# Attention and a feed-forward block on one core: late weight conversions ranked by their block, not in front of the late sweeps

## The chip, the cores and the metric

The kernel runs on one core of one Trainium2 chip. The metric is the device time of one execution in microseconds (us), median of several runs. A core has TensorE (PE, matrix products), VectorE (DVE) and ScalarE (ACT) for element work, GpSimd (POOL), and SyncE (SP), whose queue issues most of the transfers (DMA).

## What is computed

The reference, cut to its core (B = 4, H = 8, S = 1152, D = 64; 2304 tokens, model width 512, inner width 2048):

```python
q_pool = q.reshape(B, H, S // 2, 2, D).mean(axis=3)
scores = scale * np.matmul(q_pool, k.transpose(0, 1, 3, 2))
scores = scores - np.max(scores, axis=-1, keepdims=True)
attn = np.exp(scores)
attn = attn / (np.sum(attn, axis=-1, keepdims=True) + 1e-09)
x = np.matmul(attn, v)          # then heads side by side: 2304 x 512
h = x @ w_in
g = np.maximum(h, 0.0) + alpha * np.minimum(h, 0.0)
out = g @ w_out
```

## The kernel before

The first part of the program is the attention: 32 heads, each in 9 chunks of keys. Its results x go to DRAM (xs) as a high and a low half, since products are made of three matmuls in a reduced float format: high by high, high by low, low by high (`mm3`, L395).

The second part is the feed-forward block. Its inner width is cut into 16 blocks of 128 (f = 0 to 15), the tokens into 8 groups of 288 (4 batches, j = 0 or 1). For one block and one group, `hidden` (L403) makes h on PE (12 matmuls), then ACT makes pos = relu(h) and neg = relu(-h), DVE joins them with alpha (L424, called pos below), ACT rounds that to gs' high half (L430) and DVE subtracts to get the low half (L435, called gs below). With gs, PE makes y, another 12 matmuls. The low sweeps (`low_sweep`, 8 of them, blocks 0 to 4) run beside the attention and put partial sums yp into DRAM; the late or high sweeps (`high_sweep`, 8 of them, blocks 5 to 15) come after it, add up y in four PSUM banks and add yp on DVE (ys, L492). Late sweep 0 reads its x from tiles xh, late sweep 1 from tiles x.

The weights arrive as 64-bit floats, 512 KB for half a block (i = 0 is w_in, i = 1 is w_out; "half block 11.0" is block 11 with i = 0). `w_convert` (L328) turns a half block into two tiles wh and wl: a load on SP into one of two wraw tiles (L332), one step on ACT (L335), four on DVE (top L338, tail L344, sign L350, value L356), a rounding copy on ACT (wh, L317) and a subtraction on DVE (wl, L320). Blocks 0 to 4 are converted during the attention, blocks 5 to 7 at its end into tiles that the attention no longer needs, and blocks 8 to 15 (16 half blocks) after it.

The order on every engine is made when the program is built, by a list scheduler (`Scheduler`). It keeps a planned time for every engine; of the tasks that could start within a slack of the earliest one (about 200 ns on ACT and DVE, none on PE) it takes the one with the smallest `prio`. On the chip each engine then works through its own list in that order. Late sweep s has prio 2000 + s, and block f in it 0.05 (f - 5) more; y comes 0.23 behind its h. The late conversions get `2 * FF + 0.05 * (f - NLO) - HW` (L1104, FF = 1000, NLO = 5). A `lock` lets only one DVE or POOL task of a group be planned at a time.

Of the kernel before, what the change touches and what calls it, by code (L numbers as in the profile page):

```python
# [13 lines left out]
AF = mybir.ActivationFunctionType  # L14
ALU = mybir.AluOpType
# [7 lines left out]
PE, ACT, DVE, POOL, SP = range(5)  # L23
# [159 lines left out]
def attention_ffn(  # L183
# [49 lines left out]
    SWITCH: int = 9,  # L233
    GL: float = 3.5,
    COL: float = 0.099,
    HW: float = 1.0,
    XB: int = 5,
    REUSE: int = 6,
    XH: int = 1,
    RP: float = 31.0,  # L240
# [4 lines left out]
    nc = tc.nc  # L245
    NH, D, S = kt.shape
    SQ = qt.shape[4]
    B = out.shape[0]
    H = NH // B
    P = 128  # L250
    NC = S // P
    HQ = SQ // 2
# [5 lines left out]
    DMO = KD * P  # L258
# [7 lines left out]
    def act(n, psum=False):  # L266
        return n / 1.2 + (50 if psum else 93)
# [12 lines left out]
    add = sch.add  # L280
# [4 lines left out]
    nal = const.tile([P, NFF], F32, tag="nal", name="nal")  # L285
# [39 lines left out]
        add(DVE, dve(DMO), low, reads=[mag], writes=[w], deps=[t], prio=prio, lock=True)  # L325
        w_done[f, i] = w

    def w_convert(f, i, prio, release=(), ring=None, left=()):  # L328
        raw, mag, bits = Buf(r_raw), Buf(r_mag), Buf(r_bits)

        def load():
            nc.sync.dma_start(out=raw.t.rearrange("p n t -> p (n t)"), in_=wt[f, i].bitcast(I32))  # L332

        def size():
            nc.scalar.activation(out=mag.t, in_=raw.t[:, :, 1].bitcast(F32), func=AF.Abs)  # L335

        def top():
            nc.vector.tensor_scalar(  # L338
                out=bits.t, in0=raw.t[:, :, 1], scalar1=3, scalar2=0x3FFFFFF8,
                op0=ALU.logical_shift_left, op1=ALU.bitwise_and,  # L340
            )

        def tail():
            nc.vector.scalar_tensor_tensor(  # L344
                out=bits.t, in0=raw.t[:, :, 0], scalar=29, in1=bits.t,
                op0=ALU.logical_shift_right, op1=ALU.bitwise_or,
            )

        def sign():
            nc.vector.scalar_tensor_tensor(  # L350
                out=bits.t, in0=raw.t[:, :, 1], scalar=-0x40000000, in1=bits.t,
                op0=ALU.bitwise_and, op1=ALU.bitwise_or,
            )

        def value():
            nc.vector.scalar_tensor_tensor(  # L356
                out=mag.t, in0=mag.t, scalar=F64_TINY, in1=bits.t.bitcast(F32),
                op0=ALU.is_ge, op1=ALU.mult,
            )

        add(SP, 600, load, writes=[raw], prio=prio - 1, size=P * DMO * 8)
        t0 = add(ACT, act(DMO), size, reads=[raw], writes=[mag], prio=prio)
        t1 = add(DVE, dve(DMO) * 0.6, top, reads=[raw], writes=[bits], deps=release, prio=prio, lock=True)
        t2 = add(DVE, dve(DMO), tail, reads=[raw], writes=[bits], deps=[t1], prio=prio, lock=True)
        t3 = add(DVE, dve(DMO), sign, reads=[raw], writes=[bits], deps=[t2], prio=prio, lock=True)
        add(DVE, dve(DMO), value, reads=[bits], writes=[mag], deps=[t0, t3], prio=prio, lock=True)
        w_split(f, i, mag, prio, ring, left)


    nal_b = Buf()  # L370
# [32 lines left out]
    def hidden(f, x, prio):  # L403
        ps, pos, neg, gs = Buf(r_h), Buf(r_pos), Buf(r_neg), Buf(r_gs)
        t = None
        for kd in range(KD):

            def mm(kd=kd):
                mm3(ps.t, f, kd * P, lambda hl: x[kd].t[:, hl, :], kd == 0, kd == KD - 1)

            t = add(PE, 396, mm, reads=[x[kd], w_done[f, 0]], writes=[ps], deps=[t] if t else [], prio=prio,
                    kind="group" if kd else "first")
        add(
            ACT, act(HQ, True), lambda: nc.scalar.activation(out=pos.t, in_=ps.t[:, :HQ], func=AF.Relu),  # L414
            reads=[ps], writes=[pos], prio=prio,
        )
        add(
            ACT, act(HQ, True),
            lambda: nc.scalar.activation(out=neg.t, in_=ps.t[:, :HQ], func=AF.Relu, scale=-1.0),  # L419
            reads=[ps], writes=[neg], prio=prio,  # L420
        )
        t = add(
            DVE, dve(HQ),
            lambda: nc.vector.scalar_tensor_tensor(  # L424
                out=pos.t, in0=neg.t, scalar=nal[:, f:f + 1], in1=pos.t, op0=ALU.mult, op1=ALU.add
            ),
            reads=[neg, pos, nal_b], writes=[pos], prio=prio, lock=True,
        )
        t = add(
            ACT, act(HQ), lambda: nc.scalar.activation(out=gs.t[:, 0], in_=pos.t, func=AF.Copy),  # L430
            reads=[pos], writes=[gs], deps=[t], prio=prio,
        )
        add(
            DVE, dve(HQ),
            lambda: nc.vector.tensor_tensor(  # L435
                out=gs.t[:, 1], in0=pos.t, in1=gs.t[:, 0].bitcast(F32), op=ALU.subtract
            ),
            reads=[pos], writes=[gs], deps=[t], prio=prio, lock=True,
        )
        return gs  # L440
# [92 lines left out]
    pair_qs = [None]  # L533
# [20 lines left out]
                deps=deps[i], uses=[k1], writes=[k3_b[n]], prio=n - 2, size=D * S * 2,  # L554
            )

    loads = []

    def head_prep(n):
        kk, k1, q1 = Buf(r_kk), Buf(r_k1), Buf(r_q1)  # L560
        i = n % 2
        if n >= 2:
            if i == 0:
                pair_qs[0] = Buf(r_qs)
                load = add(
                    SP, 600, lambda qs=pair_qs[0]: nc.sync.dma_start(out=qs.t, in_=qt[n // 2, 0]),
                    writes=[pair_qs[0]], prio=n - Q0, size=P * 2 * SQ * 4,
                )
                add(
                    POOL, 1050,  # L570
                    lambda qs=pair_qs[0]: nc.gpsimd.dma_start(out=qs.t, in_=qt[n // 2, 1], accum_op=ALU.add),
                    writes=[pair_qs[0]], deps=[load], prio=n - Q1, size=P * 2 * SQ * 4, dma=True,
                )
            qs, qc = pair_qs[0], i
        else:
            qs, qc = Buf(r_qs), 0
            add(
                SP, 600, lambda: nc.sync.dma_start(out=qs.t, in_=qt[n // 2, :, :, i].rearrange("t d q -> d t q")),
                writes=[qs], prio=n - 2.6, size=P * 2 * SQ * 4,
            )  # L580
            eng, dur, e = pair_op(P1, SQ)
            add(
                eng, dur,
                lambda e=e: e.tensor_tensor(out=qs.t[:, 0], in0=qs.t[:, 0], in1=qs.t[:, 1], op=ALU.add),
                reads=[qs], writes=[qs], prio=n - 1.6,
            )
        for j in range(2):
            d = slice(j * D, (j + 1) * D)
            add(
                SP, 600, lambda d=d: nc.sync.dma_start(out=kk.t[d], in_=kt[n]), writes=[kk], prio=n - KL,  # L590
                size=D * S * 4,
            )
        halves(n, qs, qc, [qs.writers[-1]] * 2, n - KR)
        add(
            ACT, act(SQ), lambda: nc.scalar.activation(out=q1.t, in_=qs.t[:, qc], func=AF.Copy),
            reads=[qs], writes=[q1], prio=n - KR,
        )
        q_rest[n] = qs, qc
        add(
            ACT, act(S), lambda: nc.scalar.activation(out=k1.t, in_=kk.t, func=AF.Copy),  # L600
            reads=[kk], writes=[k1], prio=n - KR + 0.1,
        )
        loads.append(k1.writers[-1])
        key_halves(n, k1, [k1.writers] * 2)
        add(
            ACT, act(SQ),
            lambda: nc.scalar.activation(
                out=q2[n % 2][:D, PAD:], in_=q1.t[:D].bitcast(F32), func=AF.Copy
            ),
            reads=[q1], writes=[q2_b[n]], deps=old_users(n), prio=n - 0.5,  # L610
        )
        add(
            DVE, dve(S),
            lambda: nc.vector.tensor_tensor(  # L614
                out=k2[n % 2][:D], in0=kk.t[:D], in1=k1.t[:D].bitcast(F32), op=ALU.subtract
            ),
            reads=[kk, k1], writes=[k2_b[n]], deps=old_users(n) + late * (n == 1), prio=n - KS, lock=True,
        )
        return k1, q1
# [13 lines left out]
    first_q2, first_k2, first_load, late, maxed = Buf(), Buf(), [None], [], {}  # L633
# [374 lines left out]
    with ExitStack() as actx:  # L1008
# [9 lines left out]
        with ExitStack() as pctx:  # L1018
# [37 lines left out]
            for n in range(0, NH, 2):  # L1056
# [4 lines left out]
            t = add(SP, 600, lambda: nc.sync.dma_start(out=nal, in_=alpha), uses=[], writes=[nal_b], deps=[first_load[0]], prio=3)  # L1061
            add(
                DVE, 100,
                lambda: nc.vector.tensor_scalar(out=nal, in0=nal, scalar1=-1.0, scalar2=None, op0=ALU.mult),
                writes=[nal_b], deps=[t], prio=3,
            )
            for i in range(2):
                for f in range(NLO):
                    r = int(R2 + R3 * f if i else R0 + R1 * f)
                    w_convert(f, i, W2 + W3 * f if i else W0 + W1 * f, [maxed[max(0, r)]])  # L1070
            rings = [r for r in (r_kk, r_qs, r_k1) for i in range(2)]
            for c in range(REUSE):
                f, i = NLO + c // 2, c % 2
# [83 lines left out]
```

## Time and profile before

| | us |
|---|---|
| median of 3 runs (lowest, highest) | 898.33 (897.49, 900.25) |
| the profiled execution | 899.73 |
| its span, first to last instruction | 898.0 |
| PE busy | 873.2 (97%) |
| DVE busy | 622.7 (69%) |
| ACT busy | 514.2 (57%) |
| POOL busy | 171.3 (19%) |

A stage is judged by its own windows: the share of a whole span mixes the attention, in which all engines work, with the late sweeps, in which PE is nearly alone. The attention's last writes of x are issued at 553 to 556 us; late sweep 0 begins on PE at 606.25 us.

### The profile page before, as it was taken

What the parts mean: (1) busy time and instruction counts of PE and PEld (TensorE: products, weight loads), DVE (VectorE), ACT (ScalarE), POOL (GpSimd) and SP (SyncE); (2) the same over time, 40 slices, a digit from 0 to 9 for tenths busy, and PEclk for the clock granted to TensorE, in tenths of its full rate; (3) what the DMA queues carried; (4) which work ended last, traced back from release to release, by engine and by line L of the source; (5) the groups of instructions that cost most, each with busy time, mean ns of one, the idle gap of its engine ahead of it and who ended that gap; (6) DMA issues with size and microseconds to landing.
All of it is one profiled execution on the core that took longest, in us unless ns stands there. A gap on an engine that the chain in (4) does not pass through costs nothing.

```text
span 898.0 us, 16880 instructions
## 1 busy us (share of the span) xinstructions
PE 873.2 (97%) x6273; PEld 742.6 (83%) x6273; DVE 622.7 (69%) x984; ACT 514.2 (57%) x1337; POOL 171.3 (19%) x126
## 2 busy tenths in 40 slices
PE   8799899999999999999999999999899999999998
PEld 5576666677778778777777789999799999999998
DVE  6899999977887688787798972588833243243332
ACT  5577677767676677666676664565533243333432
POOL 3332333333332332333322320000000000000000
PEclk9799999999999999999999999999899999999999
DMA  9757678685755765674463435774313113112000
GB/s 261 192 153 183 161 174 221 154 223 127 186 160 131 181 171 135 152 197 131 114 148 96 115 106 146 295 229 132 118 53 107 54 54 107 53 54 93 1 27 27
DMA packets 59496, 121.71 MB, mean 136 GB/s; under 512 B 12795, under 2 KB 25622, under 8 KB 59414
## 3 DMA queue, kind: packets, MB, share of 16 engines
q1 hardware_dynamic: 57254, 111.79, 43.5%
q0 software_dynamic: 2160, 8.85, 5.6%
q8 instruction: 49, 0.80, 0.4%
q14 instruction: 33, 0.27, 0.1%
HBM read 92.36 MB, written 19.02 MB: 124 GB/s over the span
## 4 chain that ended last, share of the span: by engine, by line
PE 79%; DVE 16%; ACT 2%; issue 2%; DMA 1%; SPq 0%; POOL 0%; DVEq 0%; ACTq 0%; POOLq 0%
PE h L398 28%; PE y L398 15%; PE av L920 12%; PE s L879 7%; PE m L811 7%; PE s L880 6%; DVE bx L828 4%; PE s L942 2%; DVE acc L908 2%; DVE wmag L356 1%; DVE wl L320 1%; DVE wbits L344 1%; DVE wbits L350 1%; PE av L1043 1%; DVE k L614 1%
## 5 line engine op out<-in xcount | busy, mean ns | idle before, releaser
L892 ACT ACTIVATE p<-s 128x288 f32<-128x288 f32 x576 | 204.9, 409 | 81.1 <-PE s L880 77.1
L908 POOL TENSOR_TENSOR acc<-acc,p 128x576 f32<-128x576 f32 x96 | 151.2, 1575 | 346.6 <-ACT p L892 159.0
L828 DVE TENSOR_REDUCE bx<-m 128x2 f32<-128x768 f32 x192 | 179.9, 949 | 36.6 <-PE m L811 35.4
L879 PE MATMUL s<-q,k 128*128 128x288 f32 x576 | 171.2, 311 | 1.0 <-ACT p L892 0.8
L880 PE MATMUL s<-q,k 65*128 65x288 f32 x576 | 165.2, 300 | 0.0
L920 PE MATMUL av<-p,vv 128*64 128x288 f32 x1152 | 162.3, 417 | 0.0
L424 DVE SCALAR_TENSOR_TENSOR pos<-neg,nal,pos 128x288 f32<-128x288 f32 x128 | 66.7, 526 | 109.7 <-ACT neg L419 104.9
L879 PEld LDWEIGHTS s<-q,k 128*128 128x128 f32 x576 | 110.2, 191 | 22.4 <-issue 12.0
L414 ACT ACTIVATE pos<-h 128x288 f32<-128x288 f32 x128 | 51.3, 404 | 124.2 <-PE h L398 124.1
L920 PEld LDWEIGHTS av<-p,vv 128*64 128x64 f32 x1152 | 74.6, 137 | 55.8 <-issue 16.9
L398 PE MATMUL h<-x,wh 128*128 128x288 f32 x576 | 117.8, 297 | 0.0
L811 PE MATMUL m<-k,q 128*128 128x384 f32 (+1 forms) x384 | 106.3, 363 | 6.1 <-DVE q L627 3.6
L880 PEld LDWEIGHTS s<-q,k 65*128 65x128 f32 x576 | 110.4, 192 | 0.1
L398 PE MATMUL y<-gs,wh 128*128 128x288 f32 x512 | 105.6, 300 | 3.2 <-DVE gs L435 3.2
L398 PEld LDWEIGHTS h<-x,wh 128*128 128x128 f32 x576 | 92.3, 188 | 2.9 <-issue 2.7
L435 DVE TENSOR_TENSOR gs<-pos,gs 128x288 fp32r<-128x288 f32 x128 | 58.8, 463 | 46.0 <-ACT gs L430 45.6
L430 ACT ACTIVATE gs<-pos 128x288 fp32r<-128x288 f32 x128 | 56.2, 443 | 59.7 <-DVE pos L424 59.3
L398 PEld LDWEIGHTS y<-gs,wh 128*128 128x128 f32 x512 | 84.1, 192 | 3.7 <-DVE gs L435 3.7
L398 PE MATMUL h<-x,wl 128*128 128x288 f32 x288 | 84.8, 294 | 0.0
L811 PEld LDWEIGHTS m<-k,q 128*128 128x128 f32 (+1 forms) x384 | 62.7, 196 | 26.2 <-issue 10.0
L908 DVE TENSOR_TENSOR acc<-p 128x576 f32<-128x576 f32 x96 | 72.3, 754 | 10.9 <-ACT p L892 9.7
L398 PE MATMUL y<-gs,wl 128*128 128x288 f32 x256 | 76.5, 299 | 0.0
(97 smaller groups left out, 1263.5 us busy)
## 6 DMA issues: line engine op xcount, KB each, us to landing
kk<-kt SPq DMA_DIRECT2D x63, 288.0 KB
wraw<-wt SPq DMA_DIRECT2D x32, 512.0 KB
x<-xs SPq DMA_DIRECT2D x48, 288.0 KB
qs<-qt SPq DMA_DIRECT2D x16, 576.0 KB
vv<-vt SPq DMA_DIRECT2D x32, 288.0 KB
xs<-x SPq DMA_DIRECT2D x64, 144.0 KB
k<-k SPq DMA_DIRECT2D x62, 144.0 KB
qs<-qt POOLq DMA_DIRECT2D x15, 576.0 KB, 7.2
```

Source lines behind the costliest of these rows:

```text
L398: nc.tensor.matmul(out=ps[:, :HQ], lhsT=w[a, c // DMO][:, c % DMO:c % DMO + P], rhs=lo(hl), start=(first and i == 0), stop=(last and i == 2),)
L414: ACT, act(HQ, True), lambda: nc.scalar.activation(out=pos.t, in_=ps.t[:, :HQ], func=AF.Relu),
L424: lambda: nc.vector.scalar_tensor_tensor(out=pos.t, in0=neg.t, scalar=nal[:, f:f + 1], in1=pos.t, op0=ALU.mult, op1=ALU.add),
L430: ACT, act(HQ), lambda: nc.scalar.activation(out=gs.t[:, 0], in_=pos.t, func=AF.Copy),
L435: lambda: nc.vector.tensor_tensor(out=gs.t[:, 1], in0=pos.t, in1=gs.t[:, 0].bitcast(F32), op=ALU.subtract),
L811: nc.tensor.matmul(out=ms.t[:, i, :JW], lhsT=q1.t[d, PAD + t * P:PAD + (t + 1) * P], rhs=k1.t[d, j * JW:(j + 1) * JW], start=True, stop=True,)
L828: lambda c=c, e=e, step=step, m=len(pair), ms=ms: nc.vector.tensor_reduce(out=bx.t.rearrange("p t j -> p (t j)")[:, c:e + 1:step], in_=ms. ...
L879: nc.tensor.matmul(out=ps.t[:, :HQ], lhsT=k1.t[:, s], rhs=q1.t[:, q], start=True, stop=False)
L880: nc.tensor.matmul(out=ps.t[:, :HQ], lhsT=k2[n % 2][:, s], rhs=q2[n % 2][:, PAD + q.start:PAD + q.stop], start=False, stop=True)
L892: lambda ps=ps, p=p, h=h: nc.scalar.activation(out=p.t[:, h], in_=ps.t[:, :HQ], func=AF.Exp, scale=SCALE),
L908: lambda a=a, b=b, part=part, e=e: e.tensor_tensor(out=part.t, in0=a.t, in1=b.t, op=ALU.add),
L920: nc.tensor.matmul(out=av.t[h * D:(h + 1) * D, :HQ], lhsT=vv.t[:, e], rhs=p.t[:, h], start=(e == 0), stop=(e == NC - 1),)
```

## The change

HW goes from 1.0 to 0.1. Before, the conversions of blocks 8 to 15 had prio 1999.15 to 1999.5, ahead of everything in the late sweeps (2000 and up). Now block f's conversion has 1999.9 + 0.05 (f - 5), which is 0.1 or two blocks ahead of its own use in late sweep 0 (2000 + 0.05 (f - 5)). Loads have 1 less. Three options are new (QA, LD, NT); at their default values they leave the old branches in place, and nal gets a second operation, an addition of 0.0.

```diff
-    HW: float = 1.0,
+    HW: float = 0.1,
     XB: int = 5,
+    QA: float = 1.0,
+    LD: int = 0,
+    NT: int = 0,
...
-        add(SP, 600, load, writes=[raw], prio=prio - 1, size=P * DMO * 8)
+        add(SP, 600, load, writes=[raw], deps=first if f == 0 else (), prio=prio - 1, size=P * DMO * 8)
...
+        if not NT:
+            add(
+                ACT, act(HQ, True), lambda: nc.scalar.activation(out=pos.t, in_=ps.t[:, :HQ], func=AF.Relu),
+                reads=[ps], writes=[pos], prio=prio,
+            )
...
-                out=pos.t, in0=neg.t, scalar=nal[:, f:f + 1], in1=pos.t, op0=ALU.mult, op1=ALU.add
+                out=pos.t, in0=neg.t, scalar=nal[:, f:f + 1], in1=ps.t[:, :HQ] if NT else pos.t, op0=ALU.mult, op1=ALU.add
             ),
-            reads=[neg, pos, nal_b], writes=[pos], prio=prio, lock=True,
+            reads=[neg, ps if NT else pos, nal_b], writes=[pos], prio=prio, lock=not NT,
...
-                add(
+                q_sums[n // 2] = add(
                     POOL, 1050,
                     lambda qs=pair_qs[0]: nc.gpsimd.dma_start(out=qs.t, in_=qt[n // 2, 1], accum_op=ALU.add),
-                    writes=[pair_qs[0]], deps=[load], prio=n - Q1, size=P * 2 * SQ * 4, dma=True,
+                    writes=[pair_qs[0]], deps=[load], prio=n - Q1, size=int(QA * P * 2 * SQ * 4), dma=True,
...
-                lambda: nc.vector.tensor_scalar(out=nal, in0=nal, scalar1=-1.0, scalar2=None, op0=ALU.mult),
+                lambda: nc.vector.tensor_scalar(
+                    out=nal, in0=nal, scalar1=-1.0, scalar2=1.0 if NT else 0.0, op0=ALU.mult, op1=ALU.add
+                ),
...
-                    w_convert(f, i, W2 + W3 * f if i else W0 + W1 * f, [maxed[max(0, r)]])
+                    w_convert(f, i, W2 + W3 * f if i else W0 + W1 * f, [maxed[max(0, r)]], first=[q_sums[1]] if LD else ())
```

The lists of all engines are the same up to the end of the attention. Three places differ. In the new kernel's list the line numbers are 3 to 7 higher.

On SP, at the first weight loads of the late blocks (wraw), the list of before and the list of the change read:

```order
L462 DMA yp_0_81<-ys 128x288 x2
L332 DMA wraw<-wt 128x1024
L462 DMA yp_0_81<-ys 128x288
L332 DMA wraw<-wt 128x1024
L391 DMA xh<-xs_73 128x576
L462 DMA yp_0_81<-ys 128x288
L391 DMA x<-xs_76 128x576
L391 DMA xh<-xs_73 128x576 x3
L470 DMA ypt<-yp_0_77 128x1152
```

```order
L467 DMA yp_0_81<-ys 128x288 x2
L394 DMA xh<-xs_73 128x576
L467 DMA yp_0_81<-ys 128x288
L394 DMA xh<-xs_73 128x576 x2
L467 DMA yp_0_81<-ys 128x288
L394 DMA x<-xs_76 128x576
L394 DMA xh<-xs_73 128x576
L335 DMA wraw<-wt 128x1024 x2
L475 DMA ypt<-yp_0_77 128x1152
```

Both weight loads have moved behind the four loads of xh and one of x.

On DVE, behind the last step of half block 11.0 (wl11_0), where late sweep 0 begins (pos_7974 is block 5's, the next number block 6's), before and after:

```order
L320 TENSOR_TENSOR wl11_0_7945<-wmag_7894,wh11_0_7944 128x512
L338 TENSOR_SCALAR wbits_7986<-wraw_7887 128x512
L344 SCALAR_TENSOR_TENSOR wbits_7986<-wraw_7887,wbits_7986 128x512
L350 SCALAR_TENSOR_TENSOR wbits_7986<-wraw_7887,wbits_7986 128x512
L356 SCALAR_TENSOR_TENSOR wmag_7984<-wmag_7984,wbits_7986 128x512
L424 SCALAR_TENSOR_TENSOR pos_7974<-neg_7979,nal_68,pos_7974 128x288
L424 SCALAR_TENSOR_TENSOR pos_7996<-neg_8001,nal_68,pos_7996 128x288
L320 TENSOR_TENSOR wl11_1_8024<-wmag_7984,wh11_1_8023 128x512
L338 TENSOR_SCALAR wbits_8042<-wraw_7928 128x512
L344 SCALAR_TENSOR_TENSOR wbits_8042<-wraw_7928,wbits_8042 128x512
```

```order
L323 TENSOR_TENSOR wl11_0_7945<-wmag_7918,wh11_0_7944 128x512
L429 SCALAR_TENSOR_TENSOR pos_7974<-neg_7979,nal_68,pos_7974 128x288
L341 TENSOR_SCALAR wbits_7990<-wraw_7870 128x512
L440 TENSOR_TENSOR gs_7992<-pos_7974,gs_7992 128x288
L347 SCALAR_TENSOR_TENSOR wbits_7990<-wraw_7870,wbits_7990 128x512
L429 SCALAR_TENSOR_TENSOR pos_7998<-neg_8004,nal_68,pos_7998 128x288
L353 SCALAR_TENSOR_TENSOR wbits_7990<-wraw_7870,wbits_7990 128x512
L440 TENSOR_TENSOR gs_8019<-pos_7998,gs_8019 128x288
L359 SCALAR_TENSOR_TENSOR wmag_7985<-wmag_7985,wbits_7990 128x512
L429 SCALAR_TENSOR_TENSOR pos_8024<-neg_8032,nal_68,pos_8024 128x288
```

The hidden blocks' steps have moved in between the steps of half block 11.1. From here to the last step of half block 15.1 the list held 18 of them (pos or gs); it holds 24 now.

On PE, around the h of one of the last blocks of late sweep 0, before (wl_1_8133 and wh_1_8234 are half blocks 12.1 and 13.1, wh_0_8356 is 15.0) and after (wh_1_8275 and wh_0_8333 are 13.1 and 14.0, and h from x is late sweep 1):

```order
L398 MATMUL y<-gs,wl_1_8133 128x288
L398 MATMUL h<-xh,wh_0_8356 128x288 x2
L398 MATMUL h<-xh,wl_0_8357 128x288
L398 MATMUL h<-xh,wh_0_8356 128x288 x2
L398 MATMUL h<-xh,wl_0_8357 128x288
L398 MATMUL h<-xh,wh_0_8356 128x288 x2
L398 MATMUL h<-xh,wl_0_8357 128x288
L398 MATMUL h<-xh,wh_0_8356 128x288 x2
L398 MATMUL h<-xh,wl_0_8357 128x288
L398 MATMUL y<-gs,wh_1_8234 128x288 x2
```

```order
L401 MATMUL h<-xh,wh_0_8333 128x288 x2
L401 MATMUL h<-xh,wl_0_8334 128x288
L401 MATMUL y<-gs,wh_1_8275 128x288 x2
L401 MATMUL y<-gs,wl_1_8276 128x288
L401 MATMUL h<-x,qs 128x288 x9
L401 MATMUL h<-x,k_6829 128x288 x12
L401 MATMUL h<-x,wh_0_7493 128x288 x2
L401 MATMUL h<-x,wl_0_7494 128x288
```

Before, two hidden blocks of late sweep 1 stood ahead of late sweep 0's last y. Now seven and a quarter stand there, spread over the last blocks, and behind that y comes sweep 1's first y at once; before, three of sweep 1's hidden blocks stood between.

## Rows read from the trace of the kernel before

**Rows 1.** The page's 40 slices: the TensorE clock that was granted, in tenths.
```profile
PEclk9799999999999999999999999999899999999999
```

**Rows 2.** Windows by stage: busy PE, PEld, DVE, ACT, POOL; clock, DMA, GB/s.
```profile
550.00:600.00 50.00, 50.00 (x380) 50.00 (x379) 30.21 (x64) 28.85 (x74) 0.00 (x0) 1.00 0.73 243
...
610.00:650.00 40.00, 35.95 (x245) 35.11 (x245) 35.76 (x68) 21.97 (x54) 0.00 (x0) 0.91 0.37 114
...
700.00:880.00 180.00, 180.00 (x1363) 180.00 (x1362) 63.42 (x133) 63.27 (x171) 0.00 (x0) 1.00 0.17 55
```

**Rows 3.** Windows of 2 us behind the last conversions of late sweep 0.
```profile
638.00:640.00 2.00, 0.00 (x1) 0.01 (x1) 1.85 (x5) 0.40 (x2) 0.00 (x0) 0.79 0.00 0
640.00:642.00 2.00, 2.00 (x8) 2.00 (x9) 1.97 (x4) 1.41 (x4) 0.00 (x0) 0.50 0.02 4
```

**Rows 4.** PE's waits from 550 to 660 us: total us, times, longest us.
```profile
PE y L398 <- DVE gs L435: 3.2, 2, 3.0
PE h L398 <- ACT neg L419: 0.9, 1, 0.9
```

**Rows 5.** PE's timeline: start, us, operation, idle time before and its releaser.
```profile
606.25 1.75 PE L398 MATMUL h<-xh,kk 128*128 128x288 f32 x12
...
640.00 0.61 PE L398 MATMUL y<-gs,wh 128*128 128x288 f32 x1 [2.98 <-DVE gs L435]
...
645.68 0.57 PE L398 MATMUL h<-xh,wh 128*128 128x288 f32 x2
...
652.20 1.75 PE L398 MATMUL h<-x,k 128*128 128x288 f32 x12
```

**Rows 6.** DVE's timeline: steps with other work between them, then one half block alone.
```profile
566.22 0.42 DVE L338 TENSOR_SCALAR wbits<-wraw 128x512 int32<-128x512 int32 x1
566.56 0.51 DVE L424 SCALAR_TENSOR_TENSOR pos<-neg,nal,pos 128x288 f32<-128x288 f32 x1
566.99 0.68 DVE L356 SCALAR_TENSOR_TENSOR wmag<-wmag,wbits 128x512 f32<-128x512 f32 x1
567.59 0.45 DVE L435 TENSOR_TENSOR gs<-pos,gs 128x288 fp32r<-128x288 f32 x1
567.96 0.68 DVE L344 SCALAR_TENSOR_TENSOR wbits<-wraw,wbits 128x512 int32<-128x512 int32 x1
...
636.90 0.42 DVE L338 TENSOR_SCALAR wbits<-wraw 128x512 int32<-128x512 int32 x1
637.35 0.69 DVE L344 SCALAR_TENSOR_TENSOR wbits<-wraw,wbits 128x512 int32<-128x512 int32 x1
638.08 0.69 DVE L350 SCALAR_TENSOR_TENSOR wbits<-wraw,wbits 128x512 int32<-128x512 int32 x1
638.88 0.69 DVE L356 SCALAR_TENSOR_TENSOR wmag<-wmag,wbits 128x512 f32<-128x512 f32 x1
639.49 0.82 DVE L435 TENSOR_TENSOR gs<-pos,gs 128x288 fp32r<-128x288 f32 x2
```

**Rows 7.** DVE's timeline: the ends of half blocks 11.0 and 15.1.
```profile
606.02 0.69 DVE L320 TENSOR_TENSOR wl<-wmag,wh 128x512 fp32r<-128x512 f32 x1 [0.70 <-ACT wh L317]
...
644.33 0.68 DVE L320 TENSOR_TENSOR wl<-wmag,wh 128x512 fp32r<-128x512 f32 x1
```

**Rows 8.** All waits of DVE from 606 to 646 us.
```profile
DVE wl L320 <- ACT wh L317: 2.0, 2, 1.3
DVE wmag L356 <- ACT wmag L335: 0.8, 1, 0.8
```

**Rows 9.** SP's timeline: first weight load of the late blocks, last xh loads.
```profile
557.35 0.44 SPq L332 DMA_DIRECT2D wraw<-wt  x1
...
560.75 1.88 SPq L391 DMA_DIRECT2D xh<-xs  x3
```

**Rows 10.** DVE's timeline: the idle time after block 8's conversion.
```profile
579.86 1.13 DVE L424 SCALAR_TENSOR_TENSOR pos<-neg,nal,pos 128x288 f32<-128x288 f32 x2 [6.71 <-ACT neg L419]
```

**Rows 11.** ACT's timeline: neg of block 5 in late sweep 0.
```profile
608.34 0.40 ACT L419 ACTIVATE neg<-h 128x288 f32<-128x288 f32 x1
```

More of the change, by code (lines that the diff above doesn't have):

```diff
@@ L326, in w_split, with w_convert @@
         w_done[f, i] = w
-    def w_convert(f, i, prio, release=(), ring=None, left=()):
+    def w_convert(f, i, prio, release=(), ring=None, left=(), first=()):
         raw, mag, bits = Buf(r_raw), Buf(r_mag), Buf(r_bits)
@@ L412, in hidden @@
                     kind="group" if kd else "first")
-        add(
-            ACT, act(HQ, True), lambda: nc.scalar.activation(out=pos.t, in_=ps.t[:, :HQ], func=AF.Relu),
-            reads=[ps], writes=[pos], prio=prio,
-        )
+        if not NT:
[3 more added lines that the diff above has]
+            )
         add(
@@ L555, in key_halves @@
             )
-    loads = []
+    loads, q_sums = [], {}
     def head_prep(n):
@@ L568, in head_prep @@
                 )
-                add(
+                q_sums[n // 2] = add(
                     POOL, 1050,
                     lambda qs=pair_qs[0]: nc.gpsimd.dma_start(out=qs.t, in_=qt[n // 2, 1], accum_op=ALU.add),
-                    writes=[pair_qs[0]], deps=[load], prio=n - Q1, size=P * 2 * SQ * 4, dma=True,
+                    writes=[pair_qs[0]], deps=[load], prio=n - Q1, size=int(QA * P * 2 * SQ * 4), dma=True,
                 )
```

## The prediction

> **What bounds the kernel now.** I read the page's slices first: the clock row stands at 9 everywhere but in two slices, the second one at the start and the 29th (628.6 to 651 us), where the attention is long over [rows 1]. Then the windows by stage: TensorE (PE) is busy 50.00 of 50 us at 550 to 600 and 180.00 of 180 at 700 to 880, but only 35.95 of 40 at 610 to 650, with a mean clock of 0.91 and VectorE (DVE) busy 35.76 of 40 [rows 2]. The finer windows put the damage at 636 to 646: no matmul at 638 to 640 and a granted clock of 0.50 (1.2 of 2.4 GHz) behind it [rows 3]. The reader is to see one hole in an engine that is otherwise full. PE's waits name its cause: 3.2 us for the subtraction that makes the low half of gs (DVE, L435) and 0.9 us for ACT [rows 4].
>
> How much the hole costs comes from PE's own rows. From 606.25 (first matmul of late sweep 0) to 652.20 (first hidden block of late sweep 1 after sweep 0's last y) PE does 24 groups of 12 matmuls: 11 hidden blocks h and 11 y of sweep 0, two h of sweep 1. At full pace (180 us for 1363 matmuls [rows 2]: 0.132 us each, 1.585 per group) 24 groups take 38.0 us; they took 45.95 [rows 5]. **7.9 us are lost**: 4.1 idle, some 2.6 for 23 matmuls at half clock (640.00 to 645.68, 5.68 us against 3.04), the rest at the edges of the waits. No other stage of the late sweeps can give anything, since PE is full in them, and for the same reason what this stage gives reaches the end undiminished.
>
> Why DVE is late: each of the 16 half blocks needs five dependent operations there (0.45, 0.73, 0.80, 0.61 from start to start [rows 6], the last, wl, about 0.60 like the others: 3.19 us), and hidden blocks need pos and gs. From the end of half block 11.0 (wl at 606.02) to that of 15.1 (644.33) [rows 7] it does 9 half blocks (28.7) and 18 pos or gs (7.6 at 0.42): 36.3 of 38.3, plus 2.8 us of waits for ACT, some of it hidden [rows 8]. In that order a pair of pos or a pair of gs follows each half block, so two gs come every 8.5 us (38.3 / 9 x 2), and PE, which needs 3.2 us for a block (h and y), runs dry.
>
> **The change, part by part.** New options NT, LD and QA have values that leave their branches as they were; nal gets a second operation that adds 0.0, on one 128x16 instruction early in the kernel: nothing. Only HW acts. It adds no work and removes none: 16 half blocks, the same matmuls, the same loads. It moves three things.
>
> *Loads.* On SP the first two weight loads go behind four xh loads and one x load: from 557.35 to about 562, where today's last xh loads are out [rows 9]. If the conversion of block 8 began as late as 570, its ten steps at 0.6 would end at 576. DVE's next work starts at 579.86 after 6.71 us of idleness [rows 10], which hides the shift; without that cover it would cost DVE some 4 us. Queued behind these loads on SP are yp stores and ypt, not needed for tens of microseconds. Later loads keep their distance of two half blocks ahead of use, and DVE waited for no load [rows 8]. Zero; the bound is one missed cover, 4 us of DVE delay.
>
> *DVE order up to block 13.* The order shows that through wl of half block 11.0 little changes, so I start at 606.6. Then pos of block 5 stands directly behind it. That pos waits for ACT's neg, which starts at 608.34 and takes 0.40 [rows 11], so DVE idles 2.1 us where it now converts. Up to wl of half block 13.0 the queue holds 8 pos, 7 gs, 5 tops and 17 other conversion steps. Steps with foreign work between them cost top 0.34, pos 0.43, other steps 0.60, gs 0.37 (566.22 to 567.96 in [rows 6]): 3.44 + 2.59 + 1.70 + 10.20 = 17.9. Add 0.5 where steps still follow each other directly, 2.1 for the wait and about 1.0 for small waits on ACT: wl of 13.0 at about 628.1. PE reaches h of block 13 after 14.25 groups: 606.25 + 22.6 = 628.85. It waits for nothing, by 0.7 us.
>
> The Trainium skill ("VectorE: DVE Perf Modes", section The DRAIN you can't avoid) says that each VectorE operation waits for the pipe to empty and that a semaphore between chained operations costs nothing extra. By that rule interleaving saves nothing, the three interleaved half blocks take 1.4 us more, and the sum would be 0.7 us worse. The trace disagrees: a top is followed after 0.34 us by foreign work but after 0.45 by its own tail [rows 6].
>
> *DVE and PE order of blocks 13 to 15.* PE now does five and a quarter h of sweep 1 beyond today's two ahead of the last y. These fill what is now the hole. To wl of 15.0 DVE has 3 tops, 15 steps, 3 pos, 4 gs (1.0 + 9.0 + 1.3 + 1.5 = 12.8), 1.2 for direct succession, and two waits for h of 13 and 14 through ACT (0.8 each): 643.7. PE gets to h of 15 after 24 groups, at 644.3. To gs of 15: 6.4 more, 650.1; PE gets to that y after 28.25 groups, at 651.0. Each gate opens 0.6 to 0.9 us before PE is there. The half-block ends come later than today (15.1 at about 647.5, not 644.9); that costs nothing while PE has sweep 1's blocks. The four ys additions that free the y banks now have sweep 1's first y right behind them, where three h stood. PE comes back to a bank after 12 matmuls, 1.6 us, and an addition like gs takes 0.4: covered, if DVE reaches ys (about 651) when PE ends the first quarter of that y (651.4).
>
> **The sum.** PE's loss between 606.25 and the same point of work goes from 7.9 to something between 0 and what a late DVE leaves. Upper bound: if interleaving saved nothing and ACT's waits stayed (9 x 3.19 + 24 x 0.40 + 2.8 + 4.1 = 45.2), 15.1 would end at 651.8, 4.3 late, less the 0.6 of margin: 3.7, and 6.3 if one wait again halves the clock. My margins are smaller than my working is exact, so I take 1.0, near the lower end, since all gates come out open. Gain 7.9 - 1.0 = 6.9. The profiled execution took 899.73 (span 898.0 and 1.7 around it), 1.4 above the median of the three runs (898.33): 892.8 for a profile like it, 891.4 for the median.
>
> **Rivals.** A change below 0.3% (2.7 us) can't be told from none here.
> - *DVE a little late:* gates open 2 to 5 us after PE comes, in short waits without half clock. For it: margins under 1 us on 40 us of queue. Against: loads and ACT have slack. Loss 2.5 to 5.2, so 893 to 895.6.
> - *The hole moves:* one wait of about 3 us, at h of 13 or 15, halves the clock again, as behind the 2.98 us of idleness today [rows 5]. For it: conversions of 13 to 15 come later in DVE's queue than today. Loss 5.2 to 10.6, so 895.6 to 901.
> - *Slower, by a loop through DVE's order:* pos of block f waits for PE's h of f, the halves of f+1 stand behind that pos, and PE's next h waits for them. For it: DVE does stand idle behind one pos with other work in its list, 6.71 us up to 579.86 [rows 10]. If the three turns 12 to 15 run in series, each takes 2 x 3.19 + 4 x 0.4 + 1.6 + 0.8 = 10.4 us, while PE's filler in them is worth 6.7, 7.5 and 7.9: 9.1 lost, with a half clock 11.7, hence up to 902. It decides where a turn's length exceeds its filler by 2.6 us on average (7.9 / 3). Against it: tops and tails stand ahead of the pos in the list, so the turns overlap. The Trainium skill ("TensorE: Matmul & The Clock Gate", Engine queue depths) calls VectorE's queue a strict FIFO, the premise of this loop; the idle stretch agrees.
> - *It does nothing:* refuted by the order, except that full stages before 606 can gain nothing.
>
> **Chances.** Forecast (loss under 2.5) 0.62, DVE a little late 0.16, hole moves 0.14, slower loop 0.08. Faster 0.78, within 0.3% 0.14, slower 0.08. The likeliest range alone is 890 to 893; with the second rival and the beginning of the third 889.5 to 896.5.
>
> **What would show it.** Right: no PE wait above 1 us between 606 and 655, clock 1.00 throughout, the matmuls of sweep 1's first seven blocks before the last y of block 15, DVE with an idle stretch of about 2 us at 606.6 to 608.7, wl of 15.1 at 646 to 649, and late sweeps 1 to 7 the same length as now. Wrong: PE waiting for wl (L323 in the new lines) at h of 12 to 15, a slice of half clock, DVE waiting for a load after 560, or PE below full at 550 to 606 because the moved loads held up x or yp.

## The result, and the profile after

The changed kernel takes 889.6 us (median of 11 runs, 886.42 to 896.38), the kernel before 897.74 beside it (11 runs, 892.9 to 903.18). The ratio is 0.9915 with a 95% interval of 0.9891 to 0.994, so the change gains 7.6 us (5.4 to 9.8). The forecast was 891.4, a gain of 6.9. The measured 889.6 lies 0.1 above the lower end of the wide range (889.5 to 896.5) and 0.4 below the likeliest range alone (890 to 893): the gain was larger than forecast, and the kernel before ran 0.6 faster beside it than its earlier median of 898.33.

The profiled execution of the changed kernel is a long one, 896.38 us with a span of 894.6, only 3.4 less than the span of before. So the two spans must not be compared as they stand; the stage must. From PE's timeline, the last row of the kernel before:

```profile
893.52 0.29 PE L398 MATMUL y<-gs,wl 128*128 128x288 f32 x1
```

and four rows of the changed kernel (start, duration, operation):

```profile
610.89 1.75 PE L401 MATMUL h<-xh,kk 128*128 128x288 f32 x12
...
655.79 0.42 PE L401 MATMUL y<-gs,wh 128*128 128x288 f32 x2
...
657.40 1.75 PE L401 MATMUL y<-gs,kk 128*128 128x288 f32 x12
...
890.46 0.29 PE L401 MATMUL y<-gs,wl 128*128 128x288 f32 x1
```

The **late stage**, from the first matmul of late sweep 0 to the end of the last matmul, is 893.52 + 0.29 - 606.25 = 287.56 us before [rows 5] and 890.46 + 0.29 - 610.89 = 279.86 after: **7.70 us shorter**, which agrees with the timed 7.6. The changed kernel's execution merely entered the stage 4.64 us later (610.89 against 606.25); why is told at the end. To set its rows beside the prediction's times, 4.64 is taken off below.

The hole is gone. The page's clock slices, which had an 8 in the 29th place [rows 1]:

```profile
PEclk9999999999999999999999999999999999999999
```

and the windows by stage, as in [rows 2]:

```profile
550.00:600.00 50.00, 50.00 (x380) 50.00 (x379) 29.43 (x59) 27.73 (x71) 0.00 (x0) 1.00 0.71 235
610.00:650.00 40.00, 40.00 (x304) 40.00 (x304) 34.76 (x66) 24.19 (x57) 0.00 (x0) 1.00 0.36 114
...
700.00:880.00 180.00, 180.00 (x1363) 180.00 (x1362) 63.43 (x133) 63.28 (x171) 0.00 (x0) 1.00 0.18 55
```

PE does 304 matmuls at 610 to 650 where it did 245, at a clock of 1.00 instead of 0.91, and the same 1363 at 700 to 880. The view of PE's waits, which held 3.2 and 0.9 us [rows 4], lists nothing between 550 and 670.

DVE's waits from 602 to 656 (total, times, longest), against [rows 8]:

```profile
DVE pos L429 <- ACT neg L423: 2.7, 2, 2.1
DVE wl L323 <- ACT wh L320: 1.3, 3, 0.7
DVE gs L440 <- ACT gs L435: 0.5, 2, 0.3
```

DVE still waits, PE doesn't: DVE's waits now lie where PE doesn't need its result at once. Its timeline at the steps that the prediction timed:

```profile
584.50 1.13 DVE L429 SCALAR_TENSOR_TENSOR pos<-neg,nal,pos 128x288 f32<-128x288 f32 x2 [3.54 <-ACT neg L423]
...
613.42 0.52 DVE L429 SCALAR_TENSOR_TENSOR pos<-neg,nal,pos 128x288 f32<-128x288 f32 x1 [2.05 <-ACT neg L423]
...
632.05 0.69 DVE L323 TENSOR_TENSOR wl<-wmag,wh 128x512 fp32r<-128x512 f32 x1
...
647.83 0.69 DVE L323 TENSOR_TENSOR wl<-wmag,wh 128x512 fp32r<-128x512 f32 x1
...
651.89 0.68 DVE L323 TENSOR_TENSOR wl<-wmag,wh 128x512 fp32r<-128x512 f32 x1
...
654.26 0.89 DVE L440 TENSOR_TENSOR gs<-pos,gs 128x288 fp32r<-128x288 f32 x2
...
656.46 1.59 DVE L497 TENSOR_TENSOR ys<-y,ypt 128x288 f32<-128x288 f32 x4
```

The three wl are the ends of half blocks 13.0, 15.0 and 15.1; the second gs of the pair is what block 15's y needs. DVE has not become faster: half block 15.1 ends 651.89 + 0.68 - 610.89 = 41.68 us into the late stage, where before it ended at 644.33 + 0.68 - 606.25 = 38.76 [rows 7]. What PE does meanwhile has changed.

### The profile page after: what moved, and what is told of

Same layout as the page of the kernel before. It is cut to its first block, busy times and chain, and to the rows that moved or that the text cites. A ratio compares the mean times of both kernels' runs of the same rounds, so it can differ in the third digit from the quotient of the medians.

```text
span 894.6 us, 16888 instructions
## 1 busy us (share of the span) xinstructions
PE 874.9 (98%) x6273; PEld 742.6 (83%) x6273; DVE 622.8 (70%) x984; ACT 514.5 (58%) x1337; POOL 171.3 (19%) x126
## 4 chain that ended last, share of the span: by engine, by line
PE 82%; DVE 12%; ACT 3%; issue 2%; DMA 1%; POOL 0%; DVEq 0%; ACTq 0%; POOLq 0%
PE h L401 30%; PE y L401 16%; PE av L925 12%; PE s L884 7%; PE m L816 7%; PE s L885 6%; DVE bx L833 4%; PE s L947 2%; DVE acc L913 2%; PE av L1048 1%; ACT p L897 1%; PE m L797 1%; DVE q L632 1%; DVE k L619 1%; DVE mm L858 1%
## 5 line engine op out<-in xcount | busy, mean ns | idle before, releaser
L401 PE MATMUL y<-gs,wh 128*128 128x288 f32 x512 | 103.0, 295 | 0.0
L401 PEld LDWEIGHTS y<-gs,wh 128*128 128x128 f32 x512 | 82.1, 188 | 0.0
```

The source lines that it names most:

```text
L401: nc.tensor.matmul(out=ps[:, :HQ], lhsT=w[a, c // DMO][:, c % DMO:c % DMO + P], rhs=lo(hl), start=(first and i == 0), stop=(last and i == 2),)
```

## The experiments

Late stages are read from the same two rows of each kernel's PE timeline.

| run | ratio to before, 95% interval | late stage, from, to | PE's waits at 595 to 670 |
|---|---|---|---|
| before | 1 | 287.56 (606.25, 893.81) | 4.1 |
| after | 0.9915 (0.9891, 0.994) | 279.86 (610.89, 890.75) | none |
| e1_hw_alone | 0.9928 (0.9899, 0.9957) | 279.85 (601.86, 881.71) | none |
| e2_steps_only | 0.9914 (0.9887, 0.9941) | 279.86 (605.48, 885.34) | none |
| e3_fill2 | 0.9997 (0.9967, 1.0028) | 288.57 (605.38, 893.95) | 5.0 |
| e4_fill0 | 1.0077 (1.0048, 1.0106) | 290.13 (605.48, 895.61) | 7.5 |
| e5_keep_clock | 1.0029 (0.9996, 1.0061) | 286.59 (604.98, 891.57) | 1.1 |
| e6_hw_0p3 | 0.9951 (0.9917, 0.9984) | 281.89 (601.04, 882.93) | 1.1 |
| e7_hw_0p0 | 0.9933 (0.9905, 0.9961) | 279.74 (608.74, 888.48) | none |
| e8_hw_m0p1 | 0.9942 (0.9907, 0.9977) | 280.89 (608.04, 888.93) | 0.7 |
| e9_keep_26 | 0.9987 (0.9955, 1.0019) | 286.22 (600.56, 886.78) | 1.5 |
| e10_dve_late_2 | 0.9936 (0.9897, 0.9974) | 281.00 (602.62, 883.62) | 0.7 |
| e11_dve_late_5 | 0.9983 (0.9945, 1.0021) | 285.18 (601.56, 886.74) | 3.3 |

**Which edit acts.** e1 is the kernel before with one number changed; e2 is the kernel after with the old rank for the late loads.

```diff
-    HW: float = 1.0,
+    HW: float = 0.1,
```

> The kernel before with HW = 0.1 and nothing else of the change. Theory (the ranks are all of it): as the changed kernel, ratio to before 0.988 to 0.995, and the late stage (first matmul of late sweep 0 to the last matmul) 280 us, where before has 287.6. Rival (the second operation on nal or the new option paths move something): ratio nearer to 1.

```diff
-        add(SP, 600, load, writes=[raw], deps=first if f == 0 else (), prio=prio - 1, size=P * DMO * 8)
+        add(SP, 600, load, writes=[raw], deps=first if f == 0 else (), prio=prio - 1 - early, size=P * DMO * 8)
...
-            w_convert(f, i, 2 * FF + 0.05 * (f - NLO) - HW)
+            w_convert(f, i, 2 * FF + 0.05 * (f - NLO) - HW, early=0.9)
```

> The change, but the weight loads of blocks 8 to 15 keep their old, earlier rank; only the conversion steps get the new one. Theory (the gain comes from the order of DVE's steps): late stage 280 us, ratio 0.988 to 0.995. Rival (the move of the weight loads behind the xh loads brings part of it): late stage 282 to 286 us.

Both have after's late stage to 0.01 us. HW is the whole change, and the moved loads neither help nor hurt.

**Is it the filler?** In e3 the hidden blocks of the later sweeps, except the first two of sweep 1, wait for late sweep 0's last y; in e4 all of them do. The conversions keep their new ranks.

```diff
+            t = add(PE, 396, mm, reads=[x[kd], w_done[f, 0]], writes=[ps], deps=[t] if t else list(after), prio=prio,
...
+            gs = hidden(f, x, p, last_y if b or j and f >= NLO + FILL else ())
```

> The change, but from the third hidden block of late sweep 1 on (and in all later sweeps) h waits for late sweep 0's last y, so that two blocks of sweep 1 can fill, as many as before the change. Theory (the conversions still set the pace, and the five and a quarter more blocks of sweep 1 hide it): PE waits again, 2 to 3 us for gs of block 14 and about 2 us at block 15, loss 5.5 to 8.1 us, late stage 285 to 288 us, ratio 0.994 to 1.002. Rival (the prompt gs of late sweep 0 is the gain, the filler does little): no PE wait above 1 us, late stage 280 to 282 us, ratio below 0.994.

> As the last one, with no hidden block of late sweep 1 ahead of late sweep 0's last y. Theory: PE waits 1 to 2 us for gs of 13, about 4 us for gs of 14, 2 to 3 us for gs of 15: loss 8.7 us, or 11.3 with a stretch of half clock, late stage 288 to 292 us, ratio 1.000 to 1.006. Rival (prompt gs is the gain): late stage below 284 us, ratio below 0.997.

PE's waits in e3 (total, times, longest):

```profile
PE y L402 <- ACT gs L436: 3.1, 2, 2.2
PE y L402 <- DVE gs L441: 1.9, 1, 1.9
```

two of them in e3's PE timeline, and then the end of half block 15.0 in its DVE timeline:

```profile
642.04 0.61 PE L402 MATMUL y<-gs,wh 128*128 128x288 f32 x1 [1.90 <-DVE gs L441]
...
649.09 1.10 PE L402 MATMUL y<-gs,wh 128*128 128x288 f32 x2 [2.25 <-ACT gs L436]
```

```profile
642.32 0.69 DVE L324 TENSOR_TENSOR wl<-wmag,wh 128x512 fp32r<-128x512 f32 x1
```

With two blocks of filler the whole gain is gone: 288.57, even a little worse than before and 0.57 above the upper end that I had set. Without filler it is 290.13. DVE's conversions keep their times in after, e3 and e4: half block 15.0 ends 37.63 us into the stage in e3 (642.32 + 0.69 - 605.38) and 37.63 in after, and from 11.1 to 15.0 no end differs by more than 0.02 us in e3 or e4. So the new rank alone, without sweep 1's blocks between, buys nothing. e4's timed ratio says 6.9 us slower (4.3 to 9.5), its profile 2.6; the difference stays open.

**How the rank sets the filler.** The kernel after with other values of HW: at 0.3 four blocks of sweep 1 stand ahead of late sweep 0's last y, at 0.0 seven, at -0.1 seven and a quarter.

> The kernel after with HW = 0.3 in place of 0.1: conversions of blocks 13 to 15 rank earlier, and only 4 hidden blocks of sweep 1 (5 to 8) stand before the last y of block 15, against 7 after and 2 before. My theory (filler counted in blocks of sweep 1, the conversions set the pace): two or three blocks less filler than after, at 1.58 us each, so a loss of 3 to 5 us, late stage 282 to 285, waits of PE for the subtraction of gs or for wl. Rival (the place of the conversions in DVE's list is what matters, not the number of filler blocks): late stage within 0.5 of after's 279.86.

> The kernel after with HW = 0.0: a late block's conversion ranks with its own use, two blocks ahead no longer more than one step; 7 hidden blocks of sweep 1 (5 to 11) before the last y of block 15, as after. My theory (same filler, DVE busy throughout): late stage 279.8 to 281.5, no wait of PE above 1 us. Rival (conversions that rank this late let PE run dry at block 13 or 14, which the order puts behind one more group of y): waits for wl or ACT of 1 to 3 us, late stage 282 to 285.

> The kernel after with HW = -0.1: conversions rank behind their own use, and seven and a quarter hidden blocks of sweep 1 stand before the last y of block 15. My theory (filler is the whole cover and there is as much of it): late stage 279.8 to 282, waits if any below 1.5 us. Rival (the hole moves to the hidden blocks 13 to 15 because their conversions come last in DVE's list): waits of PE for wl or for ACT, late stage 282 to 287, perhaps with half clock.

With four blocks the stage is 2.03 us longer than after, which is not within 0.5 as the rival of e6 said; but I priced the missing blocks too high (3 to 5): PE waits only 0.9 and 0.2 us in view. The rank changes DVE's order too, so e6 alone doesn't separate filler from order. Set beside before, it does so nearly. The last end of a half block in e6:

```profile
639.14 0.69 DVE L323 TENSOR_TENSOR wl<-wmag,wh 128x512 fp32r<-128x512 f32 x1
```

That is 639.14 + 0.69 - 601.04 = 38.79 us into the stage, against 38.76 before, and no half block from 11.1 on ends more than 0.31 us from where it did before. With the conversions where they were and two more blocks of filler, 287.56 - 281.89 = 5.67 of the 7.70 us are there. So the rank acts mainly by the work that it lets in between. Seven blocks with the old ranks were not run.

At 0.0, seven blocks give the same late stage as after. At -0.1 one wait of 0.7 us for ACT appears and the stage is 1.0 longer. Of the values tried, 0.0 and 0.1 are the best and alike. The timed intervals of these three overlap, so their order rests on the profiles.

**What the half clock was worth.** The kernel before with added matmuls of 128 columns in front of block 11's y, where PE stood idle for 2.98 us; their sums go to columns of the bank that nothing reads. First 44 of them, then 26.

```diff
+                    if (b, j, f, m) == (0, 0, 11, 0):
+                        for i in range(KEEP):
+                            nc.tensor.matmul(
+                                out=y[0].t[:, HQ:HQ + P], lhsT=wh[10, 1][:, :P], rhs=x[0].t[:, 0, :P], start=False, stop=False
+                            )
```

> The kernel before, with 44 added matmuls of 128 columns (about 0.066 us each at full pace, 2.9 us in all, adding to columns of the y bank that nothing reads) in front of the y of block 11 in late sweep 0, where TensorE stood idle for 2.98 us before it ran 23 matmuls at a granted clock of 0.50. This separates the two parts of the 7.9 us. My theory (idleness brings the half clock): the idle 4.1 us stay lost, since the conversions still set the pace, but the 2.6 us of half clock go: clock 1.00 in 636 to 646, late stage (first matmul of late sweep 0 to the end of the last matmul; 287.56 before, 279.86 after) 284.5 to 285.5, ratio to before about 0.997. Rival 1 (the half clock does not come from the idle stretch): 0.50 there again, late stage 287 to 288. Rival 2 (the half clock costs nothing because the conversions would have held PE anyway): clock 1.00, but waits move behind it, late stage 286.5 to 287.6.

> The run with 44 added matmuls kept the clock at 1.00, but they took 5.03 us (0.114 each) where the idle stretch was 2.98, so its late stage (286.59) holds 2 us that are not the kernel's. 26 of them take 26 x 0.114 = 2.97 us and should fit the stretch. Theory (idle time of 4.1 and half clock of 2.6 are two separate parts of the 7.9 us, and idleness brings the second): granted clock 1.00 at 636 to 646, late stage 287.56 - 2.6 = 284.5 to 285.3, ratio to before 0.996 to 0.998. Rival (the half clock came for another reason, or the conversions hold PE up anyway): late stage 286.5 to 287.6, ratio 1.0.

e9's PE timeline, from the added matmuls on:

```profile
631.00 3.01 PE L485 MATMUL y<-xh,wh 128*128 128x128 f32 x26
633.85 0.86 PE L399 MATMUL y<-gs,wh 128*128 128x288 f32 x2
...
637.48 0.43 PE L399 MATMUL h<-xh,wh 128*128 128x288 f32 x2
...
639.76 0.41 PE L399 MATMUL y<-gs,wh 128*128 128x288 f32 x1 [0.40 <-DVE gs L436]
...
643.10 0.90 PE L399 MATMUL y<-gs,wh 128*128 128x288 f32 x2
```

The clock in both runs, e5 first (PEclk is the column behind POOL's):

```profile
610.00:650.00 40.00, 38.86 (x297) 38.25 (x296) 35.96 (x68) 21.46 (x52) 0.00 (x0) 1.00 0.36 119
```

```profile
610.00:650.00 40.00, 38.25 (x282) 36.74 (x281) 34.70 (x67) 20.43 (x51) 0.00 (x0) 1.00 0.42 138
```

It stays at 1.00, where before had 0.91 [rows 2]: the idleness brought the half clock. From the place of block 11's y to block 15's h it now takes 637.48 - 631.00 = 6.48 us where before it took 645.68 [rows 5] less 636.72, the start of that y, 8.96. So 2.48 us come back, as the 2.6 of the prediction said. But the late stage shrinks by 1.34 only. The other half is lost again by block 15's y: PE arrives earlier at the y of blocks 13 and 15 and waits there for gs (the 0.40, and the pair of 0.90, where a pair without a wait takes 0.43). The pair of 0.86 at 633.85 is block 11's own y, which waits out the end of the hole. My theory in e9 (284.5 to 285.3) missed, and so did its rival's range (286.5 to 287.6): 286.22 lies between, and each mechanism was half right. In e5 the added matmuls took 5.03 us instead of the 2.9 that I had estimated and overran the hole by 2 us, which makes its ratio useless.

**The margin, and the loop through DVE.** The kernel after with one conversion step of half block 12.0 done again three or seven times (the same bits); every list stays.

```diff
+            for _ in range(AGAIN + 1 if (f, i) == (12, 0) else 1):
                 nc.vector.scalar_tensor_tensor(
                     out=bits.t, in0=raw.t[:, :, 1], scalar=-0x40000000, in1=bits.t,
```

> The kernel after, with one VectorE step of half block 12.0 (sign, which gives the same bits again) done four times: some 2.2 us more (3 x 0.73) ahead of the conversions of 12 to 15, every list otherwise as after. This measures the margin. Theory (PE meets its gates with about 0.8 us to spare at block 13 and 0.4 to 0.5 at block 15, and a delay reaches the end once): PE waits 1.2 to 1.8 us in all, late stage 281.1 to 281.7 against 279.86. Rival 1 (the loop through VectorE's list: a late pos makes the next halves late, so the delay is paid anew at blocks 13, 14 and 15): 3 us or more, late stage 283 or more. Rival 2 (more slack than worked out): late stage within 0.5 of 279.86.

> The same with the step done eight times, some 5 us more. Theory: PE waits 4 to 4.8 us in all, late stage 283.9 to 284.7, and 2.6 more if the longest wait again brings a stretch of half clock. Rival 1 (the loop pays it anew at each of three blocks): 8 us or more, late stage 288 or more. Rival 2 (more slack): late stage below 283.

The added steps in e10's DVE timeline, and its one PE wait:

```profile
613.54 2.87 DVE L355 SCALAR_TENSOR_TENSOR wbits<-wraw,wbits 128x512 int32<-128x512 int32 x4
```

```profile
619.63 0.40 PE L403 MATMUL h<-xh,wl 128*128 128x288 f32 x1 [0.68 <-DVE wl L324]
```

Three more steps take 2.87 - 0.69 = 2.18 us and the late stage grows by 1.14, so the margin at h of block 12 is 1.04; blocks 13 to 15 pay nothing more. The 281.00 lies 0.1 below my range, and the wait in view is 0.68, not 1.2 to 1.8. In e11 (seven steps, 5.1 us) PE waits 2.28 and 1.04 us at the same h:

```profile
619.91 0.53 PE L403 MATMUL h<-xh,wh 128*128 128x288 f32 x2 [2.28 <-ACT wh L321]
621.49 0.61 PE L403 MATMUL h<-xh,wl 128*128 128x288 f32 x1 [1.04 <-DVE wl L324]
```

and the window behind them shows 1.2 of 2.4 GHz:

```profile
622.00:624.00 2.00, 2.00 (x10) 2.00 (x9) 2.00 (x6) 1.64 (x3) 0.00 (x0) 0.50 0.70 250
```

The stage grows by 5.32: 5.1 less 1.04 of margin, 4.1, and the rest, 1.2, is of the size of that stretch of half clock: 13 matmuls from 621.49 to 624.71 took 3.22 us, at full pace 1.72. I had set 2.6 for such a stretch, so the 285.18 falls between my two ranges (283.9 to 284.7 without, 286.5 to 287.3 with it): this stretch was shorter than that of before. A delay reaches the end once. The loop that pays it anew at each of three blocks would have shown 288 or more.

## Why the prediction was right

- **The bound** was right. The hole's 7.9 us were worked out from 24 groups of matmuls; 7.70 came back, and PE has no wait left in the stage.
- **Loads at zero** held: the first weight load is issued at 566.26 in the changed kernel, 561.6 with 4.64 taken off (predicted about 562), DVE still had 3.54 us of idleness behind block 8's conversion, of the 6.71 that were to hide the shift [rows 10], and e2 gives the same late stage without the move. The one wait of DVE that is put down to a transfer, 0.17 us at 578.28, lies ahead of that idleness and costs nothing. The issue's row on SP:

```profile
566.26 1.17 SPq L335 DMA_DIRECT2D wraw<-wt  x2
```

- **DVE's order** held to half a microsecond. The wait for block 5's neg is 2.05 us (predicted 2.1). With 4.64 taken off, wl of 13.0 ends at 628.1 (predicted 628.1), wl of 15.0 at 643.9 (643.7), gs of block 15 at 650.5 (650.1), wl of 15.1 at 647.9 (about 647.5); PE comes to block 15's y at 651.15 (651.0). A sum of single rows, each by its own price with or without foreign work between, predicted 40 us of a queue. That wl of 13.0 fits to 0.1 is in part luck: of the 1.0 set for small waits on ACT, 0.5 show as waits, and the other half lies in small gaps between steps.
- **The rule from the Trainium skill** ("VectorE: DVE Perf Modes", The DRAIN you can't avoid), as the prediction took it, would have had interleaving save nothing, and wl of 13.0 come 1.4 us later. It came at 628.1, so the rows' price stands here. The same section also says that a next operation which isn't held starts earlier; the prediction left that out, and no run here tells which operations were held.
- **The filler** is the cause: e3 takes it away, with every conversion up to 15.0 where it was, and the gain goes with it; e6 has two blocks more than before, with the conversions of before, and has most of the gain.
- **The y banks** turned in time: the four ys start at 656.46 while block 15's y still runs, and sweep 1's first y follows at 657.40 without a gap.
- **The loss term was mis-sized.** I took 1.0 us for what a late DVE leaves. It is about 0.2: from 610.89 to 657.40 PE does 29.25 groups in 46.51 us, where 1.585 each make 46.36. The gain was 7.7, not 6.9. The margins came as predicted (0.6 to 0.9): 0.8 at h of block 13 (wl ends at 632.74, h starts at 633.54) and 0.6 at y of block 15 (655.15 against 655.79). I took their smallness for a risk, but a gate that opens in time costs nothing.
- **The split of the 7.9** into 4.1 of idleness and 2.6 of half clock was right as a reading but not as two sums that can be had apart: e9 got 2.48 back at the spot and kept 1.34. The prediction's sum didn't need the split.
- **The rivals.** No wait of PE in after, so neither "DVE a little late" nor "the hole moves" came. The loop through DVE's order falls with e10 and e11. The prediction's reason, that tops and tails stand ahead of the late pos and so turns overlap, fits but was not tested by itself. The late sweeps 1 to 7 stayed as they were (1363 matmuls at 700 to 880 in both).

The forecast for a profile like that of before, 892.8, doesn't match the profiled 896.38: that execution entered the late stage 4.64 us later, and it was late already at its first matmul for scores (21.19 against 15.33), long before the lists differ.

## What to carry to other kernels

When a full engine has one hole, count what its list holds until the late producer is done: moving independent work of the next pass into that stretch can be worth the hole, although the producer gets no faster. Rank a long preparation by the use of each of its parts, not as one block in front, and check with the rows' own prices that each part still arrives in time. When an idle stretch and a clock fall stand in one sum, what keeping the clock returns must be tested at the next gate, since the producer behind it may take it back.

## What was not expected of the hardware

**The start differs between executions of one program.** Windows of the start-up, the kernel before:

```profile
8.00:12.00 4.00, 4.00 (x17) 2.81 (x17) 3.91 (x5) 3.26 (x7) 2.45 (x3) 1.00 1.01 263
12.00:16.00 4.00, 4.00 (x22) 2.52 (x20) 3.28 (x7) 1.31 (x2) 0.59 (x1) 1.00 1.05 401
```

and the kernel after:

```profile
8.00:12.00 4.00, 4.00 (x9) 2.27 (x9) 2.55 (x3) 3.26 (x7) 2.46 (x3) 1.00 1.00 253
12.00:16.00 4.00, 4.00 (x11) 2.52 (x11) 1.88 (x3) 0.96 (x1) 0.61 (x1) 1.00 1.05 400
```

The lists of both are the same there, yet 39 matmuls against 20 are done in 8 us, with PE busy throughout. The first matmul for scores takes 0.44 us at 21.19 in the changed kernel, like those at 1.2 GHz in e11, and 0.29 at 15.33 in the kernel before. In the changed kernel these matmuls keep the longer duration until 24.54:

```profile
24.54 0.44 PE L885 MATMUL s<-q,k 65*128 65x288 f32 x1
...
25.66 0.29 PE L884 MATMUL s<-q,k 128*128 128x288 f32 x1
```

The clock column says 1.00 from 0 to 40 us of this execution, so at the start it doesn't agree with the durations. e7 and e8 started slowly too (9 matmuls at 8 to 12; the other runs 13 to 17), and these three entered the late stage at 608.0 to 610.9, all others at 600.6 to 606.3. That this spread explains the 10 us between executions of one kernel is likely, not shown; why a start is slow stays open.

**Which idleness halves the clock.** Half clock stood behind 2.98 us of idleness [rows 5], behind 1.90 that followed 0.82 and behind 2.25 in e3, and behind 1.04 that followed 2.28 in e11. In e4, 2.14 us up to 639.65 did not bring it at once; behind 2.08 more, up to 642.13, it stood. Windows of 2 us in e4:

```profile
640.00:642.00 2.00, 0.05 (x1) 0.00 (x0) 1.86 (x5) 0.26 (x1) 0.00 (x0) 0.98 0.00 0
642.00:644.00 2.00, 1.87 (x8) 1.87 (x9) 1.97 (x5) 0.95 (x2) 0.00 (x0) 0.50 0.04 8
```

The 40 slices of e4's page hide this stretch (a 9 in each slice of the late stage); windows of 2 us show it.
